# A state update in two wide operations instead of four narrow ones, r and k of two chunks scaled together, and a new written order

## The chip, the cores and the metric

The kernel runs on one core of one Trainium2 chip. The metric is the device time of one execution in microseconds (us). Three runs of the kernel before took 506.49, 506.82 and 509.15 us, median 506.82.

## The reference

Two stages, in float32. The first is a linear attention with a decaying state: for each of 4 batches and 8 heads (head size 48, 768 positions)

```
for t in range(S):
    cur = u[None] * kt  (outer)  vt
    y[t] = rt @ (state + cur)
    state = w * state + kt (outer) vt
```

The second is a feed-forward on the 3072 resulting rows of 384: `h = x @ w_in` (384 to 2048), `g = h * erf(softplus(h))`, `out = g @ w_out` (2048 to 384).

## The kernel before

The attention is computed in 24 chunks of 128 positions; a chunk of number g belongs to batch g % 4. Heads stand in four pairs: of a pair, head one lies on partitions 0 to 47 and head two on 64 to 111, so a pair fills `PR` = 112 rows. The steps of one chunk, each with a letter in the written order (the number behind the letter is the chunk's):

- `L..a`, `L..b`: SP loads the two halves of a chunk into a tile `att` (three buffers, a fourth for chunk 3). The `a` half holds r and k transposed (2 x 512 columns), the `b` half v, k and r in natural layout.
- `R`, `K`, `N` (lines 224 to 234): r, k and natural k are scaled by tables of powers of w (`wr`, `wk`, `wkn`). A `+` behind a word puts a step on POOL, a `*` on ACT, nothing on DVE.
- `A` (line 298): TensorE forms the 128x128 scores. `Qa`, `Qb`, `Qc`, `M` make the diagonal tile `am`, `P` copies the masked scores into it. Chunks 0 and 1 go another way (`G`, `V`, `Q`): line 322 masks the scores and line 338 adds the diagonal.
- `Y` (line 331): output of the chunk, from `am` and from the state `sbd`. `Xa`, `Xc`, `Xb` split it in a high and a low part for the feed-forward.
- `D` (line 356): TensorE forms the chunk's own contribution `ds` to the state, 112 rows by 4 pairs by 48 columns in PSUM.
- `S` (lines 370 to 380): the state update. The state tile `sbd` has 112 rows, 4 batches, 4 pairs and 96 columns and is block-diagonal: head one uses columns 0 to 47 of rows 0 to 47, head two columns 48 to 95 of rows 64 to 111; the rest is zero. Each update works on the two blocks apart, 48 rows and 192 columns: for chunks 0 to 3 two multiplies on DVE (`Sc`, `Sd`), for the later ones two adds on DVE (`Sa`, `Sb`) and two multiplies on DVE or POOL (`Sc`, `Sd`).

The feed-forward goes in 96 steps n of 512 rows by 128 hidden columns: `f` (line 412) 9 matmuls into a PSUM tile `h` (three buffers, which `ds` and the later `y` share), then `a b z c d e g h l` (five activations and a cast on ACT, three operations on DVE), then `p` (line 467) 9 matmuls into the accumulators. The float32 weights are fetched (`F`) and split in two parts (`Ca`, `Cc`, `Ce`, `Cf`) on the way.

All of this is put in one written order: the string `ORDER`, line 727, is read word for word, and each engine executes its instructions in that order. An instruction that waits holds back all that follow on its engine. 16 dummy matmuls run on TensorE while the first loads land (line 510, `W2` is two more).

```
pw (tables of powers)  ->  R, K  ->  A  ->  P  ->  Y  ->  X  ->  f0  ->  a0 b0 z0 c0 d0 e0 g0 h0 l0  ->  p0
```

Of the kernel before, what the change touches and what calls it, by code (L numbers as in the profile page):

```python
# [9 lines left out]
F32 = mybir.dt.float32  # L10
# [29 lines left out]
V0, K0, R0, AW = 1024, 1472, 1856, 2240  # L40
# [3 lines left out]
def body(ctx: ExitStack, tc: tile.TileContext, att, attn, wcol, ucol, u, win, wout, levels, outT):  # L44
    nc = tc.nc
# [118 lines left out]
    wr = const.tile([PR, NPAIR, C], F32, name="wr")  # L164
    wk = const.tile([PR, NPAIR, C], F32, name="wk")
# [374 lines left out]
    preps = dict(K=prep_k, R=prep_r, N=prep_n, G=prep_g)  # L540
    words = ORDER.split()
    last = max(i for i, x in enumerate(words) if x[0] == "C")
    for i, x in enumerate(words):
# [60 lines left out]
        elif what == "S":  # L604
            if sub in "ab":
                s_add(num, "ab".index(sub))
            elif num < 4:
                s_add(num, "cd".index(sub))
            else:
                s_mul(num, "cd".index(sub), eng)  # L610
# [122 lines left out]
C02a d1 e1 L7a C01f f2 N6 S4b C02c f3 g1 P50 a2 h1 P51 Y5 S4d+ M60+ F03 L7b F11 b2 z2 M61* a3 b3 C02e R6+ K6 l1 A6 Q7a
Q7b z3 X5a c2 X5b P60 d2 c3 d3 e2 e3 C11a P61 Q7c g2 C02f+ g3 M70 C11c p1 f4 h2 l2 a4 b4 C11e K7+ R7+ C11f+ M71+ N7+
Y6 D6 A7 S6b S6a f5 z4 F12 C03a X6a c4 d4 e4 a5 h3 P70 X6b C03c P71 b5 C03e C03f+ g4 l3 z5 p2 Y7 D7 C12a X7a h4 c5 d5
e5 S7b S6c+ N5+ S7a X7b C12c S4c L10a F13 F05 L8a C12e C13a p3 f6 f7 a6 C12f+ g5 l4 b6 z6 h5 l5 C13c c6 a7 d6 b7 z7 e6
g6 f8 p4 p5 f9 a8 c7 C13e h6 l6 L8b F04 b8 C05a z8 R10+ C13f d7 c8 d8 e7 e8 g7 a9 h7 g8 C05c l7 p6 f10 b9 h8 l8 C05e
p7x a10 b10 z10 z9 O70a F14 O70b p7y O71a c10 d10 c9 e10 p7z p8x f11 p8y d9 e9 O72a a11 g10 C05f+ g9 h9 C04a b11 Q8a+
Q8b Q8c l9 M80 f12 a12 z11 C04c O72b O71b F07 L10b p8z h10 l10 c11 d11 b12 z12 e11 C14a c12 p9 f13 d12 a13 e12 g11 b13
h11 g12 l11 p10 f14 f15 p11 z13 h12 l12 a14 C04e b14 z14 C04f C14c c13 d13 c14 e13 a15 d14 g13 M81 F06 b15 e14 C07a  # L740
h13 C14e g14 l13 z15 C14f p12 f16 f17 h14 a16 c15 l14 p13 d15 b16 C07c z16 e15 a17 c16 g15 h15 l15 F15 C07e d16 b17 R8
C07f K10+ K8+ e16 g16 z17 p14 p15x O150a p15y O151a D5 A8 S5b Q10a+ h16 C06a c17 d17 l16 S5a C06c C06e e17 g17 L9a
O150b f18 a18 p15z b18 f19 h17 O152a P80 l17 z18 p16x C06f+ p16y p16z f20 p17 a19 b19 c18 z19 C15a d18 P81 e18 c19 d19
g18 C15c e19 C15e h18 a20 f21 L9b O152b F16 O151b O230a O231a F17 b20 Q9a+ Q10b+ Q9b Q10c g19 h19 a21 C16a l18 C15f+
z20 l19 Q9c M90+ c20 b21 d20 e20 z21 g20 C16c f22 c21 a22 d21 e21 p18 N8 g21 p19 f23 f24 C16e h20 C16f l20 h21 b22 z22
C17a R9+ N9 l21 a23 c22 b23 K9 z23 d22 e22 c23 g22 C17c p20 d23 e23 C17e g23 h23 a24 C17f+ M91+ p21 Y8 h22 l22 X8a b24
f25 a25 A9 b25 M100* X8b l23 z24 z25 S7d+ S5d+ M101+ S5c+ c24 d24 e24 c25 d25 D8 p22 p23x L11a L11b P90 S8a P91 g24
# [12 lines left out]
X13b M151* g42 p41 D13 Y14 D14 A15 X14a h42 S13a S13b S14b l43 S14a P150 l42 f44 a44 f45 p42 b44 z44 X14b P151 p43 Y15  # L760
# [98 lines left out]
```

## Time and profile before

| | |
|---|---|
| profiled execution, its own time | 506.56 us |
| span in the profile | 504.7 us |
| PE busy | 491.9 us (97%) in 4466 matmuls |
| ACT busy | 393.0 us (78%) |
| DVE busy | 344.5 us (68%) in 622 operations |
| POOL busy | 133.8 us (27%) |
| DMA moved | 48.15 MB |
| chain that ended last | PE 87%, DVE 5%, ACT 5%, DMA 1% |

1.86 us of the execution lie outside the span. Busy shares are of the whole span; the page gives the granted clock of TensorE as full in all 40 slices. A matmul's end is modelled, so what counts on PE is when the next instruction starts and what is named as the reason of an idle time.

### The profile page before, as it was taken

The page shows a single profiled execution, that of the slowest core. Times are in us where ns is not written, and L with a number is a line of the kernel's source. Part 1 is how long each engine was busy: PE and PEld are TensorE (multiplying, and loading weights), DVE is VectorE, ACT ScalarE, POOL GpSimd, SP SyncE. Part 2 cuts the span into 40 slices and gives each one's busy share as a digit, 9 for nine tenths or more (in the row PEclk, how much of TensorE's full clock was granted, in tenths as well). Part 3 has the DMA queues.
Part 4 walks back from the last instruction along what each step waited for, and adds up shares of the span by engine and source line. Part 5 has one row for each costly group of instructions (what it writes and reads, how often), then busy time and mean ns, then how long its engine had stood idle before and what let it go on. Part 6 is the DMA issues. An engine that isn't in the chain of part 4 may idle for free.

```text
span 504.7 us, 11016 instructions
## 1 busy us (share of the span) xinstructions
PE 491.9 (97%) x4466; PEld 392.6 (78%) x4466; DVE 344.5 (68%) x622; ACT 393.0 (78%) x714; POOL 133.8 (27%) x126
## 2 busy tenths in 40 slices
PE   7899999999999999999999999999999999999995
PEld 4867887887878888887888878778878788888883
DVE  7999875687978967665777768677664444445452
ACT  1768999999986676878678875877786878988783
POOL 5755744103354453200171033436000000000000
PEclk9999999999999999999999999999999999999999
DMA  7966462436305521300430122322010000100001
GB/s 266 357 223 219 169 216 84 154 124 198 126 10 188 193 105 44 112 1 1 169 129 1 43 92 92 114 94 93 22 42 1 1 1 1 42 22 0 0 1 68
DMA packets 14136, 48.15 MB, mean 95 GB/s; under 512 B 1792, under 2 KB 2176, under 8 KB 14080
## 3 DMA queue, kind: packets, MB, share of 16 engines
q1 hardware_dynamic: 14080, 47.39, 26.8%
q8 instruction: 37, 0.61, 0.5%
q14 instruction: 19, 0.16, 0.1%
HBM read 41.09 MB, written 6.29 MB: 94 GB/s over the span
## 4 chain that ended last, share of the span: by engine, by line
PE 87%; DVE 5%; ACT 5%; DMA 1%; issue 1%; SPq 0%; DVEq 0%; ACTq 0%
PE h L419 38%; PE acc L479 37%; PE y L338 6%; PE A L309 3%; PE ds L361 1%; DMA att<-in_att_dram 1%; DVE s L435 1%; ACT s L439 1%; DVE s L451 1%; DVE gl L462 1%; ACT s L443 1%; ACT am L289 1%; ACT gh L457 1%; ACT s L447 1%; DVE am L317 1%
## 5 line engine op out<-in xcount | busy, mean ns | idle before, releaser
L419 PE MATMUL h<-x,wih 128*128 128x512 f32 x576 | 183.1, 399 | 0.6 <-ACT x L400 0.3
L419 PEld LDWEIGHTS h<-x,wih 128*128 128x128 f32 x576 | 107.4, 188 | 27.5 <-PE A L309 0.6
L479 PE MATMUL acc<-gh,woh 128*128 128x512 f32 x288 | 115.6, 401 | 0.1
L479 PE MATMUL acc<-gl,woh 128*128 128x512 f32 x288 | 114.4, 397 | 0.5 <-DVE gl L462 0.5
L419 PE MATMUL h<-x,wil 128*128 128x512 f32 x288 | 114.2, 396 | 0.0
L479 PE MATMUL acc<-gh,wol 128*128 128x512 f32 x288 | 114.1, 396 | 0.0
L451 DVE SCALAR_TENSOR_TENSOR s<-s,h 128x512 f32<-128x512 f32 x96 | 65.2, 684 | 64.6 <-ACT s L447 64.4
L462 DVE TENSOR_TENSOR gl<-s,gh 128x512 fp32r<-128x512 f32 x96 | 71.8, 754 | 42.0 <-ACT gh L457 40.1
L435 DVE SCALAR_TENSOR_TENSOR s<-s,h 128x512 f32<-128x512 f32 x96 | 65.5, 685 | 35.3 <-ACT s L430 33.5
L426 ACT ACTIVATE s<-h 128x512 f32<-128x512 f32 x96 | 56.4, 588 | 34.3 <-PE h L419 33.2
L439 ACT ACTIVATE s<-s 128x512 f32<-128x512 f32 x96 | 60.1, 627 | 29.0 <-DVE s L435 28.9
L457 ACT CAST gh<-s 128x512 fp32r<-128x512 f32 x96 | 58.5, 614 | 17.1 <-DVE s L451 12.0
L479 PEld LDWEIGHTS acc<-gh,woh 128*128 128x128 f32 x288 | 54.2, 188 | 14.6 <-issue 0.9
L479 PEld LDWEIGHTS acc<-gl,woh 128*128 128x128 f32 x288 | 54.3, 188 | 13.8 <-DVE gl L462 1.3
L419 PEld LDWEIGHTS h<-x,wil 128*128 128x128 f32 x288 | 54.2, 188 | 13.3 <-DVE wil L142 0.2
L479 PEld LDWEIGHTS acc<-gh,wol 128*128 128x128 f32 x288 | 54.2, 188 | 13.0
L430 ACT ACTIVATE s<-s 128x512 f32<-128x512 f32 x96 | 60.2, 628 | 1.6
L443 ACT ACTIVATE s<-s 128x512 f32<-128x512 f32 x96 | 60.0, 627 | 1.8
L447 ACT ACTIVATE s<-s 128x512 f32<-128x512 f32 x96 | 59.8, 627 | 1.8
L317 DVE COPY_PREDICATED am<-mask,A 64x128 f32<-64x128 uint32 (+2 forms) x108 | 37.9, 388 | 2.4 <-POOL am L530 0.9
L530 POOL TENSOR_TENSOR att<-att,ub 128x384 f32<-128x384 f32 x15 | 17.1, 1138 | 63.3 <-DMA att<-in_att_dram 62.8
L530 POOL TENSOR_TENSOR att<-att,wk 112x512 f32<-112x512 f32 x14 | 18.4, 1317 | 51.2 <-DMA att<-in_att_dram 50.4
(88 smaller groups left out, 460.9 us busy)
## 6 DMA issues: line engine op xcount, KB each, us to landing
att<-in_att_dram SPq DMA_DIRECT2D x22, 608.0 KB, 5.6
att<-in_att_dram SPq DMA_DIRECT2D x24, 512.0 KB, 3.9
raw<-in_wout_dram SPq DMA_DIRECT2D x8, 768.0 KB, 4.4
raw<-in_win_dram SPq DMA_DIRECT2D x7, 768.0 KB, 4.3
out_dram<-o SPq DMA_DIRECT2D x18, 256.0 KB, 2.3
part<-o SPq DMA_DIRECT2D x6, 256.0 KB, 3.0
o<-part SPq DMA_DIRECT2D x6, 256.0 KB, 3.4
raw<-in_win_dram SPq DMA_DIRECT2D x2, 384.0 KB, 9.0
```

What stands on the lines that cost most here:

```text
L317: nc.vector.copy_predicated(out=o, data=ap[rows, n, :, i], mask=mask[rows, n, None, i].to_broadcast(list(o.shape)).bitcast(U32))
L419: nc.tensor.matmul(out=h, lhsT=w[:, f, q, :], rhs=x[:, xi, q, :], start=k == 0, stop=k == 8)
L426: nc.scalar.activation(out=s1, in_=e["h"], func=AF.Tanh, bias=FB0, scale=FA0 * SHIFT)
L430: nc.scalar.activation(out=s1, in_=s1, func=AF.Tanh, bias=FB1, scale=FA1)
L435: nc.vector.scalar_tensor_tensor(out=e["s"], in0=e["s1"], scalar=FG / SHIFT, in1=e["h"], op0=ALU.mult, op1=ALU.add)
L439: nc.scalar.activation(out=s, in_=s, func=AF.Tanh, bias=FB2, scale=FA2 * SHIFT)
L443: nc.scalar.activation(out=s, in_=s, func=AF.Square, bias=FB3, scale=FA3)
L447: nc.scalar.activation(out=s, in_=s, func=AF.Square, bias=FB4, scale=FA4)
L451: nc.vector.scalar_tensor_tensor(out=s, in0=s, scalar=FC, in1=ff[n]["h"], op0=ALU.subtract, op1=ALU.mult, reverse0=True)
L457: nc.scalar.copy(out=e["gh"], in_=e["s"])
L462: eng.tensor_tensor(out=e["gl"], in0=e["s"], in1=e["gh"].bitcast(F32), op=ALU.subtract)
L479: nc.tensor.matmul(out=acc[e], lhsT=w[:, f, es], rhs=g, start=first and i == 0, stop=last and i == 2)
```

## The change

1. `sbd` is updated over all 112 rows and 384 columns at once. The contribution `ds` is read twice over (a broadcast over the two 48-column blocks), and the multiply uses a new table `own` that holds w to the 128th power in the own block and zero in the other, so the other block returns to zero. For chunks 0 to 3 that is one multiply (`Sc`), for the later ones one add (`Sa`, DVE) and one multiply (`Sc`, DVE or POOL). So that no row is undefined, the eight of a chunk's sixteen `ds` matmuls that have 16 columns become four of 32 and four of 16.
2. `wr` and `wk` become one tile `wrk`. Chunks 0 and 1 have r and k scaled by one operation of 1024 columns (`J`).
3. `ORDER` is written anew.

```
-    wr = const.tile([PR, NPAIR, C], F32, name="wr")
-    wk = const.tile([PR, NPAIR, C], F32, name="wk")
+    wrk = const.tile([PR, 2, NPAIR, C], F32, name="wrk")
+    wr, wk = wrk[:, 0], wrk[:, 1]
...
+    own = const.tile([PR, NPAIR, 2], F32, name="own")
+    nc.gpsimd.memset(own, 0.0)
...
+    for r, hh in ((slice(0, D), 0), (slice(H, PR), 1)):
+        nc.gpsimd.tensor_copy(out=own[r, :, hh], in_=wp[r, 7, 0])
...
+    def prep_both(g, eng):
+        t = chunks[g][:PR, 0:V0]
+        eng.tensor_tensor(out=t, in0=t, in1=wrk.rearrange("p n a c -> p (n a c)"), op=ALU.mult)
...
-            for c0, c1 in ((0, 32), (32, D)):
+            for c0, c1 in ((0, 32), (32, D if hh else H)):
...
-    def s_add(g, hh):
...
-    def s_mul(g, hh, eng):
...
+    def s_wide(g, part, eng):
+        sv = sbd[:, g % 4].rearrange("p a (n d) -> p a n d", n=2)
+        if part == "a" or g < 4:
+            ds = st_[g]["ds"][:, :, None, :].to_broadcast([PR, NPAIR, 2, D])
+        if part == "a":
+            nc.vector.tensor_tensor(out=sv, in0=sv, in1=ds, op=ALU.add)
         else:
+            eng.tensor_tensor(out=sv, in0=ds if g < 4 else sv, in1=own[:, :, :, None].to_broadcast([PR, NPAIR, 2, D]),
+                              op=ALU.mult)
...
-L0a U0 L1a L2a L0b L2b F00 L3a L1b F08 L3b B0 B0* H0 R0 K0 A0 K1 G0 V0 W2 R1 A1 R2 F10 G1+ P00 Q0 P01 K2 P10 Q2a+ Q2b+
...
+L0a L1a L2a U0 L0b L2b L3a L3b L1b F00 B0 B0* J0 A0 G0 V0 J1 P00 P01 Q0 A1 Y0 Q2a P10 P11 R2+ K2+ G1+ H0 N0* D0 X0a V1
...
```

Counted over the whole program, PE issues the same number of matmuls, `W2` included; DVE loses 38 operations, ACT 12, POOL gains 6. On ACT the diagonal tiles `M` fall from 12 to 9, each of four activations. On DVE 40 adds and first multiplies of the state become 20; the 32 later multiplies (17 on POOL, 15 on DVE) become 16 (9 and 7).

The order moves the most in front of `f0`. Three places:

On DVE, the stretch in which the states of chunks 0 and 1 are written (`sbd<-ds`), before:

```order
L261 TENSOR_TENSOR att_172<-att_172,kt_261 128x4x48 x2
L374 TENSOR_TENSOR sbd<-ds_244,wp 48x4x48
L278 TENSOR_REDUCE q_307<-att_174 128x8
L374 TENSOR_TENSOR sbd<-ds_244,wp 48x4x48
L291 TENSOR_TENSOR am_0_310<-idents,q_307 128x512
```

and now:

```order
L282 TENSOR_TENSOR att_176<-att_176 128x384
L385 TENSOR_TENSOR sbd<-ds_269,own 112x384
L286 TENSOR_REDUCE q_315<-att_176 128x8
L238 TENSOR_TENSOR att_181<-att_181,wrk 112x512
L269 TENSOR_TENSOR att_174<-att_174,kt_288 128x4x48 x2
L282 TENSOR_TENSOR att_181<-att_181 128x384
L385 TENSOR_TENSOR sbd<-ds_333,own 112x384
```

The two narrow writes around the reduce are one wide write, and the work of chunk 3 (`att_181`) has moved in between.

On ACT, the last operations in front of the first activation of the feed-forward (`x` are the halves of the attention's output, `am` the diagonal tiles, `top` a weight group), before:

```order
L289 ACTIVATE am_0_415<-idents,q_398 128x128 x4
L289 ACTIVATE am_1_420<-idents,q_398 128x128 x4
L400 CAST x_407<-y_270 128x3x128
L400 CAST x_407<-y_322 128x3x128
L130 ACTIVATE top<-raw_228 128x768
L383 CAST x_407<-y_475 128x3x128
L383 CAST x_407<-y_492 128x3x128
L400 CAST x_407<-y_475 128x3x128
L400 CAST x_407<-y_492 128x3x128
L426 ACTIVATE s_0_554<-h_544 128x512
```

and now:

```order
L297 ACTIVATE am_1_391<-idents,q_381 128x128 x4
L406 CAST x_286<-y_350 128x3x128
L140 CAST wih<-wt_384 128x384
L130 ACTIVATE top<-raw_458 128x768
L389 CAST x_286<-y_440 128x3x128
L389 CAST x_286<-y_468 128x3x128
L297 ACTIVATE am_1_524<-idents,q_511 128x128 x4
L406 CAST x_286<-y_440 128x3x128
L406 CAST x_286<-y_468 128x3x128
L140 CAST woh<-wt_518 128x768
L432 ACTIVATE s_0_563<-h_552 128x512
```

A diagonal tile of chunk 4 (`am_1_524`) now stands in front of the last two casts of `x`, and a weight group `top<-raw_458` still in front of the first two.

On SP, the loads behind the first halves of the chunks, before:

```order
L75 DMA att_174<-in_att_dram 128x1216
L120 DMA raw_178<-in_win_dram 128x1536
L71 DMA att_180<-in_att_dram 128x1024
L75 DMA att_172<-in_att_dram 128x448
L120 DMA raw_178<-in_win_dram 128x1536
L75 DMA att_180<-in_att_dram 128x1216
L120 DMA raw_228<-in_wout_dram 128x3072
```

and now:

```order
L75 DMA att_176<-in_att_dram 128x1216
L71 DMA att_181<-in_att_dram 128x1024
L75 DMA att_181<-in_att_dram 128x1216
L75 DMA att_174<-in_att_dram 128x448
L120 DMA raw_185<-in_win_dram 128x1536 x2
L71 DMA att_310<-in_att_dram 128x1024
L75 DMA att_310<-in_att_dram 128x1216
L120 DMA raw_458<-in_wout_dram 128x3072
```

Chunk 3 now comes ahead of the first weights, and chunk 4 (`att_310`, which takes over the buffer of chunk 0) ahead of the weight group `raw_458` that ACT's `top` reads.

## Rows read from the trace of the kernel before

**Rows 1.** Busy time by stage; columns: window, then PE, PEld, DVE, ACT, POOL, PEclk, DMA
```profile
8.80:27.40 18.60, 16.80 (x418) 14.66 (x417) 17.89 (x34) 11.22 (x30) 11.56 (x9) 1.00 0.91 335
27.40:41.30 13.90, 12.68 (x214) 9.05 (x213) 13.50 (x23) 8.91 (x15) 8.02 (x6) 1.00 0.66 235
41.30:317.00 275.70, 275.48 (x2565) 222.62 (x2564) 207.67 (x365) 227.30 (x410) 93.40 (x79) 1.00 0.32 111
317.00:323.00 6.00, 4.86 (x128) 3.80 (x127) 3.75 (x8) 5.39 (x12) 1.66 (x2) 1.00 0.10 17
490.00:504.70 14.70, 8.64 (x36) 6.17 (x34) 4.74 (x7) 5.80 (x10) 0.00 (x0) 0.95 0.16 58
```
**Rows 2.** Timeline of PE, head: start, us, operation xcount [idle before <-releaser]
```profile
8.84 1.16 PE L309 MATMUL A<-att 48*128 48x128 f32 x16
10.41 1.02 PE L247 MATMUL kt<-uw,att 112*128 112x2 f32 x8 [0.41 <-DVE att L239]
...
19.65 0.54 PE L361 MATMUL ds<-att 128*16 128x48 f32 x30 [1.10 <-issue]
...
24.45 1.95 PE L338 MATMUL y<-am,att 128*32 128x128 f32 x64
...
28.13 0.50 PE L419 MATMUL h<-x,wih 128*128 128x512 f32 x1 [0.29 <-ACT x L400]
...
34.52 0.86 PE L338 MATMUL y<-att,sbd 112*32 112x128 f32 x24 [0.46 <-DVE sbd L374]
...
38.11 0.50 PE L479 MATMUL acc<-gl,woh 128*128 128x512 f32 x1 [0.23 <-DVE gl L462]
...
41.30 0.63 PE L419 MATMUL h<-x,wih 128*128 128x512 f32 x2
```
**Rows 3.** Waits of PE, whole span: engine, line, waited for, us in total, times, longest
```profile
PE ds L361 <- DVE s L451: 0.9, 1, 0.9
```
**Rows 4.** Timeline of DVE, head
```profile
6.60 0.68 DVE L230 TENSOR_TENSOR att<-att,wr 112x512 f32<-112x512 f32 x1
7.20 0.68 DVE L226 TENSOR_TENSOR att<-att,wk 112x512 f32<-112x512 f32 x1
...
17.38 0.36 DVE L374 TENSOR_TENSOR sbd<-ds,wp 48x192 f32<-48x192 f32 x1
17.77 0.79 DVE L291 TENSOR_TENSOR am<-idents,q 128x512 f32<-128x512 f32 x1
...
22.16 2.62 DVE L317 COPY_PREDICATED am<-mask,A 128x512 f32<-128x512 uint32 x4 [0.25 <-PE A L309]
```
**Rows 5.** Groups by shape, whole span: operation, shapes xcount, busy us, mean ns, idle before
```profile
L530 POOL TENSOR_TENSOR att<-att,ub 128x384 f32<-128x384 f32 x15 | 17.1, 1138 | 63.3 <-DMA att<-in_att_dram 62.8
L530 POOL TENSOR_TENSOR sbd<-sbd,wp 48x192 f32<-48x192 f32 x17 | 11.3, 664 | 4.9 <-DVE sbd L376 3.7
L376 DVE TENSOR_TENSOR sbd<-sbd,ds 48x192 f32<-48x192 f32 x32 | 11.2, 350 | 2.2 <-PE ds L361 1.7
L386 DVE TENSOR_TENSOR x<-y,x 128x384 fp32r<-128x384 f32 x20 | 11.0, 550 | 1.7 <-ACT x L383 1.6
```
**Rows 6.** Timeline of ACT, head
```profile
21.54 2.45 ACT L289 ACTIVATE am<-idents,q 128x128 f32<-128x128 f32 x8
...
24.62 1.11 ACT L130 ACTIVATE top<-raw 128x768 f16<-128x768 bf16 x1
```
**Rows 7.** Busy time by stage, two later windows (columns as in rows 1)
```profile
70.00:100.00 30.00, 30.00 (x129) 24.02 (x129) 19.33 (x29) 28.69 (x52) 6.93 (x6) 1.00 0.40 140
100.00:145.00 45.00, 45.00 (x275) 35.94 (x277) 36.76 (x56) 44.33 (x77) 8.68 (x7) 1.00 0.38 126
```
**Rows 8.** DMA issues by line: KB each, median us from issue to landing
```profile
raw<-in_wout_dram SPq DMA_DIRECT2D x8, 768.0 KB, 4.4
raw<-in_win_dram SPq DMA_DIRECT2D x2, 384.0 KB, 9.0
```
**Rows 9.** Timeline of SP, the issue of chunk 4's first half
```profile
17.06 0.33 SPq L71 DMA_DIRECT2D att<-in_att_dram  x1
```

More of the change, by code (lines that the diff above doesn't have):

```diff
@@ L604, in body @@
         elif what == "S":
[L605 to L610, printed above, removed]
+            s_wide(num, sub, eng)
         elif what == "F":
@@ L733 @@
[L733 to L747, printed above, removed]
@@ new lines @@
+f16 a16 p12 c15 h14 l14 b16 d15 z16 p13 f17 C07e F15 F06 c16 e15 g15 R8+ d16 a17 h15 p14 A8 D5 b17 e16 l15 z17 g16
+C06a p15x c17 C07f+ h16 O150a C06c S5a P80 l16 d17 C06e e17 C06f+ g17 P81 Q10b O150b L9a L9b F16 p15y O151a p15z f18
+f19 f20 K9+ S5c+ R9+ a18 C15a C15c b18 z18 a19 h17 l17 O152a c18 b19 z19 p16x p16y d18 p16z p17 O151b F17 O152b O230a
+O231a e18 a20 c19 Q9a+ g18 h18 d19 e19 C15e b20 f21 l18 g19 h19 a21 C16a b21 C15f Q10c l19 z20 Q9b C16c z21 Q9c N9+
+N8+ M90+ f22 a22 c20 d20 c21 e20 d21 C16e e21 g20 g21 p18 h20 b22 l20 C16f p19 f23 f24 z22 C17a a23 h21 C17c l21 c22
@@ new lines @@
+b23 M91 z23 C17e d22 e22 p20 p21 g22 c23 d23 e23 C17f g23 h23 h22 l23 l22 f25 a25 a24 Y8 A9 b24 b25 z24 z25 X8a c24
+d24 e24 X8b P90 P91 g24 p22 p23x p23y p23z D8 h24 c25 d25 e25 Y9 O231b S8a g25 D9 X9a h25 S9a M100 M101+ S7c+ K10+ A10
+O230b l24 X9b l25 f26 f27 a26 b26 N10 z26 P100 P101 a27 b27 z27 c26 p24x p24y f28 d26 e26 c27 O231c L11a L11b O232a
+L12a O232b p24z R11+ Q11a Q11b+ d27 N11+ R12+ O230c L12b K12+ Q12a+ Q12b+ e27 g26 K11 h26 a28 g27 l26 Q11c b28 z28
+M110 c28 M111* p25 Y10 D10 A11 p26 S10a P110 P111 Y11 O232c O310a O311a L13a X10a d28 e28 h27 L13b S8c g28 X10b Q12c
@@ new lines @@
+Q16c M160+ Q17a+ M161+ g45 X15a h45 D15 A16 S15a X15b P160 l45 L18a L18b O311c f46 a46 f47 f48 b46 z46 Q17b h44 l44
+p44 p45 c46 d46 e46 a47 b47 a48 Q18a z47 N17+ S15c+ g46 Q17c N16+ c47 d47 e47 h46 b48 g47 h47 M170+ M171+ Q18b+ l46
+Q18c f49 f50 a49 b49 p46 z48 l47 p47x z49 p47y p47z c48 d48 e48 a50 c49 P161 g48 d49 e49 h48 R18+ K17+ R17+ l48 b50
+O470a g49 z50 O471a h49 l49 S13c f51 a51 b51 z51 p48x f52 p48y O470b O472a c50 c51 d50 e50 d51 e51 p48z p49 g50 g51
+h50 l50 Y16 D16 A17 L19a L19b a52 b52 S16a z52 K18 h51 X16a X16b Z0a P170 l51 c52 p50 f53 f54 d52 a53 b53 P171 e52 z53
@@ new lines @@
+c68 d68 e68 d67 e67 a69 g68 h68 g67 p66 Y23 Y22 X23a h67 X23b l68 X22a b69 X22b z69 l67 f70 f71 c69 d69 a70 b70 z70
+e69 p67 c70 d70 a71 g69 b71 h69 l69 f72 a72 z71 c71 d71 e70 p68 p69 e71 g70 g71 h71 l71 b72 h70 z72 l70 f73 Z0b f74
+p70 c72 a73 d72 e72 b73 a74 g72 Z0c z73 c73 h72 b74 d73 l72 p71 f75 O632b z74 e73 g73 c74 d74 h73 e74 a75 b75 g74 l73
+z75 c75 f76 p72 p73 f77 d75 e75 a76 g75 b76 h75 l75 h74 z76 l74 c76 d76 a77 b77 f78 z77 e76 g76 p74 f79 p75 c77 a78
+d77 e77 b78 h76 a79 g77 l76 z78 b79 c78 h77 d78 e78 l77 z79 g78 f80 a80 p76 p77 f81 b80 c79 d79 h78 l78 e79 g79 h79
@@ new lines @@
+z80 c80 d80 e80 a81 l79 g80 f82 b81 a82 p78 p79x p79y z81 b82 c81 h80 l80 O790a d81 O791a e81 z82 g81 p79z f83 p80x
+p80y f84 c82 d82 h81 a83 e82 b83 l81 g82 z83 O791b O790b O792a c83 p80z p81 f85 h82 l82 a84 b84 d83 e83 z84 g83 h83
+c84 d84 a85 b85 l83 z85 c85 d85 e84 e85 g84 g85 p82 p83 f86 a86 h84 f87 f88 b86 h85 l84 z86 l85 a87 c86 d86 a88 b88
+e86 p84 g86 h86 b87 z88 l86 z87 p85 f89 p86 c88 c87 d87 e87 d88 e88 g87 g88 f90 f91 a89 h87 l87 b89 h88 z89 l88 c89
+a90 d89 b90 z90 e89 g89 p87 c90 d90 e90 a91 b91 h89 l89 g90 p88 f92 f93 h90 a92 b92 l90 z91 z92 c91 d91 a93 e91 p89
@@ L790 @@
+g91 c92 h91 l91 d92 b93 z93 e92 g92 c93 p90 f94 f95 d93 e93 h92 l92 g93 a94 b94 z94 a95 b95 c94 p91 h93 l93 d94 z95
+p92 e94 g94 c95 h94 l94 d95 e95 g95 p93 p94 h95 l95 p95x O950a p95y p95z O792b O951a O952a O950b O951b O952b
 """
```

87 lines of the change are left out of this document (33 added, 54 removed).

## The prediction, made before the changed kernel ran

> **What bounds the kernel now.** I read the busy time by stage first, then the timeline of PE where the stages show idle time, and then the engines that PE waits for there. In the stages [rows 1] PE is idle for 1.80 us of the first 18.60 after the dummies (18.60 - 16.80), for 1.22 of the next 13.90, for 0.22 of the 275.70 that follow, and for 1.14 between 317 and 323 us. From the first scores to the last matmul that is 4.4 us. The rest of the idle time is the start, in which PE runs dummies until 8.84 us, and the 6.06 us of the last stage, mostly the way of the last output to memory. So PE, in the order in which it is told to work, is the bound; DVE, ACT and POOL matter only where PE waits for them. By the counts given with the change, PE issues as many matmuls as before. Everything that this change can win is therefore in those 4.4 us (0.9%), and 3.0 of them lie between 8.8 and 41.3 us.
>
> The timeline of PE names them [rows 2]: 0.41 us in front of the first `kt`, whose operand DVE made late; 1.10 us in the middle of `ds` of chunk 1, released by nothing that the profile shows ("issue"); 0.29 us inside `f0`, for the last cast of `x`; 0.46 us in front of `Y4`, which waits for a state write on DVE; 0.23 us in `p0`, for the low half `gl`; the rest in pieces under 0.25. At 41.30 us `f2` starts; by then PE has done `A0` to `A5`, `Y0` to `Y4`, `D0` to `D4`, `f0`, `f1` and `p0`. The new order has done exactly this set when its `f2` starts, `W2` included, so the start of `f2` is a mark at which both can be compared: what moves it is idle time alone. The 1.14 us at 317 hang on a PSUM buffer that DVE frees with a `g` step, 0.9 of them [rows 3].
>
> **The change part by part.**
>
> *One scaling for r and k.* Before: two operations of 0.68 us that overlap by 0.08 [rows 4], 1.28 together. One of 1024 columns is bounded by 1.28 and, without any saving, 1.36. It ends by 6.60 + 1.36 = 7.96 us, while PE runs dummies until 8.84 [rows 2]: nothing gained, nothing lost. Behind it the product for `kt` comes next on DVE (0.68 us, so 8.6), no longer behind chunk 1, and PE reaches `kt` at 8.84 + 1.16 = 10.0. The wait of 0.41 goes.
>
> *The wide state update.* The trace has no such operation. The nearest rows are a PSUM source of 384 columns on all rows, 0.55 us [rows 5], and a product with a broadcast operand on 512 columns, 0.79 us [rows 4]. Two narrow ones cost 2 x 0.35 = 0.70 [rows 5]. So one update costs DVE between 0.15 less and 0.09 more; I take 0.55, the row with the same columns and the same source. Over 20 updates that is 3.0 us less DVE work (bounds: 3.0 less to 1.8 more). From 41 to 317 us it hides behind PE, which has 0.22 us of idle time there [rows 1]; it costs or gives only in the head, where DVE is busy for 13.50 of 13.90 us [rows 1], and there it is four or five updates, 0.7 us. Behind a narrow write on the upper rows the trace shows no overlap: the one at 17.38 is 0.36 long and the next starts at 17.77, while two operations on all rows overlap by 0.08 [rows 4]. The Trainium skill has a rule for this ("VectorE: DVE Perf Modes", section on two Vector instructions with no wait between them): an instruction whose operands start in another quadrant of partitions than those of the one before is held until that one has finished. The trace agrees with it at this place. By that rule the head would save some 0.1 us more on each side of every second narrow write; if that reached PE in part, the sum would be some 0.3 us lower. I leave it out.
>
> The later multiplies: on POOL nine of about 1.14 us (the row with 384 columns) take the place of seventeen of 0.66, 10.3 us for 11.3 [rows 5]. They wait for nothing that PE is about to use, and POOL sits idle for most of the span. I cost them at zero.
>
> *The wider `ds` matmuls.* 20 chunks times 4, in two passes each, 160 instructions grow from 16 to 32 columns. The row of `ds` shows 30 in 0.54 us, 18 ns each, both widths mixed [rows 2]. If time went by width, they would be 24 and 12, and the change would cost 160 x 12 ns = 1.9 us on PE itself. The other end is nothing, because the 48 moving columns are the same. I take nothing, and keep 1.9 for the range.
>
> *The order in the head.* What idle time is left, if PE does the same work? (a) The 1.10 us of "issue" came among the many small matmuls of the first two chunks, and the new order issues the same ones there: I keep it. (b) `Y2` and `Y3` need four masked copies, 2.62 us on DVE [rows 4], which start when `A2` is done. Meanwhile PE has `A3` (as long as `A0`, 1.16) and `Y2` (half of 1.95 [rows 2]), together 2.1, and a subtraction of `x`; `D2` no longer stands in front. The fourth copy ends between 0 and 0.5 us after that: I take 0.25. (c) `f0` needs the low halves of `x`. On ACT there stand, from the end of `Y3`: a cast, four activations for a diagonal tile (half of 2.45, 1.23 [rows 6]), two casts; with a cast at no more than DVE's 0.55 for the same columns [rows 5] that is at most 2.9 us. PE covers `D2` 0.54 and `A4` 1.16 [rows 2] of them, 1.7 us, and two subtractions of `x` and the first matmul of `f0`. The wait lies between 0 and 1.2 us; I take 0.3, what the same matmul waited before for the same cast [rows 2]. (d) The waits of `Y4` and `p0` (0.46 and 0.23) go, since `Y4` now stands in front of `f1` but its state writes come before the first feed-forward step on DVE, and since the two dummies `W2`, which used to run while PE had to wait anyway, now stand in front of `p0` and give `gl` 0.5 us. The sum: 1.10 + 0.25 + 0.3 = 1.65 us instead of 3.02, a gain of 1.4.
>
> *Whether it is kept.* From 70 to 145 us ACT is busy for 28.69 of 30 and 44.33 of 45 us [rows 7]; it has 2.0 us to spare in 75 (1.31 + 0.67). If PE is 1.4 us early, ACT has to be as well. Counted in the two orders from `a0` to `h22`, ACT now has one diagonal tile (1.23 us [rows 6]) and one weight cast less. That is about the gain, so I count it as kept. Past 145 us nothing is priced.
>
> The profiled execution took 506.56 us, 0.26 under the median of 506.82: 506.56 - 1.4 = **505.2 us**.
>
> **The rivals.**
>
> *ACT takes it back.* ACT is nearly full up to 145 us [rows 7]. If the diagonal tile's work is not enough, PE meets its 1.4 us as waits in front of `p` steps there, and the time is that of before, 506.6. For it: 2.0 us of slack in 75. Against it: the tile and the cast that are gone.
>
> *The two odd waits do not come back.* The 1.10 us of "issue" [rows 2] and the 0.9 us for the PSUM buffer [rows 3] each happened once. In another order both may miss: 505.2 - 1.10 - 0.9 = 503.2. The Trainium skill ("Runtime: NRT & Kernel Launch", section on instruction fetch mechanics) says that an engine's program is streamed in 16 KiB blocks and that this is mostly hidden. By that rule the 1.10 us is no toll for instructions and need not return; no row here shows what PE waited for. Against this rival: (a) above.
>
> *The weight group comes late: slower.* On SP, chunk 4 now stands ahead of the weight group that ACT's `top` reads, and chunk 4 waits for the buffer of chunk 0: its issue was at 17.06 us [rows 9]. With three issues of 0.33 the weights go out at about 18.1. In front of ACT's casts of `x`, `top` started at 24.62 before [rows 6]. The landing takes 4.4 us by the same tensor's row, or 9.0 by the slowest weight row, in this stretch [rows 8]: 22.5 or 27.1. From 24.6 on each microsecond holds the casts and `f0` by as much: 27.1 gives 505.2 + 2.5 = 507.7, and with the dearer `ds` matmuls 509.6. Against it: chunk 0 is needed less long in the new order (its `Y0` stands right behind `A1`), so the issue should come earlier.
>
> **How the numbers follow.** 0.5% is 2.5 us, about what a measurement of this kernel can tell from no change. Forecast 0.38 (504.2 to 506), ACT takes it back 0.19 (506 to 507), the odd waits gone 0.27 (502.4 to 504.2), the late weights 0.16 (507 to 509.8). Faster by over 2.5 us (under 504.3): nearly all of the third and a little of the first, 0.28. Slower (over 509.3): a good half of the last, 0.09. Same: 0.63. The range leaves out the lower end of the third case and the upper part of the last: 502.6 to 508.6.
>
> **What would show it.** `f2` should start near 39.9 us instead of 41.30; the `kt` step should have no wait; an "issue" gap of about 1 us should again stand among the small matmuls before 25 us; the wide updates should take about 0.55 us on DVE and 1.14 on POOL; 32-column `ds` steps should still take 0.54. From 41 to 317 us PE should stay idle for under half a microsecond. The prediction is wrong if `f2` starts as forecast but PE waits for `gh` or `gl` later, if `top` stands waiting for a DMA before `f0`, or if idle time of over 1 us shows up past 145 us, in a part for which I priced nothing.

## The result, and the profile after

The changed kernel took 501.38 us (median of 4 runs, 500.35 to 502.27) against 507.79 for the kernel before in the same job (506.49 to 509.15): a ratio of 0.987, 95% interval 0.983 to 0.992. It is 3.8 us faster than forecast, and below the range. In the later jobs the kernel before took 506.9 to 507.5 us in the median and spread from 505 to 512 over 88 runs; the changed kernel, run again, took 501.12 (500.97 to 502.13). In those 88 runs the time goes with the mean granted clock of TensorE: the 46 with 0.996 or more took 505.97 us in the median, the 8 under 0.989 took 510.2. So there are two results: the time falls by 1.3%, and the spread falls from 7 us to under 2, as far as nine runs of the changed kernel show it (e12 below, the same kernel with its tiles 32 bytes further on, reached 503.47 in six).

The busy time by stage of the changed kernel (profiled execution: 500.35 us, span 498.5), cut as in [rows 1]:

```profile
8.80:27.40 18.60, 17.99 (x448) 15.36 (x446) 18.46 (x34) 11.79 (x32) 12.61 (x10) 1.00 0.90 337
27.40:41.30 13.90, 13.81 (x196) 10.52 (x195) 13.56 (x22) 11.07 (x18) 9.53 (x8) 1.00 0.79 307
41.30:317.00 275.70, 275.60 (x2675) 222.97 (x2674) 197.85 (x335) 224.62 (x393) 105.65 (x83) 1.00 0.31 107
317.00:323.00 6.00, 6.00 (x27) 4.82 (x27) 5.80 (x10) 3.85 (x10) 2.89 (x3) 1.00 0.55 191
```

PE is idle for 0.61 and 0.09 us in the two stages of the head (1.80 and 1.22 before), and the 1.14 us at 317 are gone. PE's timeline in the head, to be read beside [rows 2]:

```profile
8.42 1.16 PE L317 MATMUL A<-att 48*128 48x128 f32 x16
9.52 1.05 PE L255 MATMUL kt<-uw,att 112*128 112x2 f32 x8
...
21.94 0.64 PE L346 MATMUL y<-am,att 128*32 128x128 f32 x15 [0.20 <-DVE am L325]
22.90 1.40 PE L346 MATMUL y<-am,att 128*32 128x128 f32 x43 [0.32 <-issue]
...
26.53 0.89 PE L425 MATMUL h<-x,wih 128*128 128x512 f32 x2
...
29.34 0.83 PE L346 MATMUL y<-att,sbd 112*32 112x128 f32 x24
...
35.70 0.50 PE L485 MATMUL acc<-gl,woh 128*128 128x512 f32 x1
...
37.67 0.63 PE L425 MATMUL h<-x,wih 128*128 128x512 f32 x2
```

The mark, the start of `f2`, falls from 41.30 to 37.67 us (in a second profile of each kernel, taken later, it stands at 43.10 and 38.22). Of these 3.63 us, 0.42 are the earlier first scores (8.84 to 8.42), and 2.33 are idle time between matmuls (gaps over 50 ns: 3.02 before, 0.69 now). The remaining 0.9 shows from start to start alone, with those gaps left out: the 160 `ds` matmuls up to the mark take 2.75 us before and 2.25 now, the two dummies of `W2` 0.53 and 0.26. The last matmul ends 6.29 us earlier, so another 2.66 come after `f2`. The wait at 317 is 1.0 of them (two gaps, 0.15 and 0.88). The rest is no wait at all: the mean distance of the starts of neighbouring feed-forward matmuls (`f` and `p` steps, some 1,670 pairs, those over 300 ns left out) falls from 234.24 to 233.38 ns, and with 1,728 such matmuls that is 1.5 us. This mean distance is called the pitch below.

DVE's timeline in the head, and POOL's at two places of it:

```profile
8.46 1.22 DVE L230 TENSOR_TENSOR att<-att,wrk 112x1024 f32<-112x1024 f32 x1
...
14.77 0.54 DVE L385 TENSOR_TENSOR sbd<-ds,own 112x384 f32<-112x384 f32 x1
...
18.55 1.01 DVE L136 SCALAR_TENSOR_TENSOR wt<-raw,top 128x384 int32<-128x384 int32 x2
...
20.55 2.58 DVE L325 COPY_PREDICATED am<-mask,A 128x512 f32<-128x512 uint32 x4
```

```profile
8.64 3.53 POOL L536 TENSOR_TENSOR att<-att,wrk 112x512 f32<-112x512 f32 x2 [0.77 <-DVE att L247]
...
20.06 1.44 POOL L536 TENSOR_TENSOR att<-att,ub 128x384 f32<-128x384 f32 x1 [1.48 <-PE A L317]
```

The new operations by shape (busy us, mean ns), beside [rows 5]:

```profile
L536 POOL TENSOR_TENSOR sbd<-sbd,own 112x384 f32<-112x384 f32 x9 | 8.9, 992 | 3.7 <-DVE sbd L383 3.0
L383 DVE TENSOR_TENSOR sbd<-sbd,ds 112x384 f32<-112x384 f32 x16 | 8.7, 551 | 5.4 <-PE ds L369 5.4
L230 DVE TENSOR_TENSOR att<-att,wrk 112x1024 f32<-112x1024 f32 x2 | 2.4, 1222 | 0.1
L385 DVE TENSOR_TENSOR sbd<-ds,own 112x384 f32<-112x384 f32 x4 | 2.2, 544 | 0.0
```

### The profile page after: what moved, and what is told of

Same layout as the page of the kernel before. It is cut to its first block, busy times and chain, and to the rows that moved or that the text cites. A ratio compares the mean times of both kernels' runs of the same rounds, so it can differ in the third digit from the quotient of the medians.

```text
span 498.5 us, 10972 instructions
## 1 busy us (share of the span) xinstructions
PE 489.1 (98%) x4466; PEld 391.7 (79%) x4466; DVE 334.2 (67%) x584; ACT 390.6 (78%) x702; POOL 149.9 (30%) x132
## 3 DMA queue, kind: packets, MB, share of 16 engines
HBM read 41.09 MB, written 6.29 MB: 95 GB/s over the span
## 4 chain that ended last, share of the span: by engine, by line
PE 92%; DVE 4%; ACT 2%; issue 1%; DVEq 0%; ACTq 0%
PE h L425 39%; PE acc L485 39%; PE y L346 7%; PE A L317 4%; PE ds L369 1%; PE dummy L95 1%; DVE gl L468 1%; DVE am L325 1%; DVE s L457 1%; DVE s L441 1%; DVE wt L136 1%; PE kt L255 0%; ACT gh L463 0%; ACT L89 0%; ACT s L453 0%
## 5 line engine op out<-in xcount | busy, mean ns | idle before, releaser
L536 POOL TENSOR_TENSOR att<-att,wrk 112x512 f32<-112x512 f32 x28 | 41.3, 1476 | 42.3 <-DMA att<-in_att_dram 39.9
L536 POOL TENSOR_TENSOR am<-idents,q 128x512 f32<-128x512 f32 x22 | 25.4, 1156 | 54.2 <-issue 24.3
```

Of the source, the lines that this page charges most:

```text
L536: i = nc.gpsimd.tensor_tensor(**kw)
```

## The experiments

**Which part of the change brings the gain?** Four kernels mix the old and the new. All four have the changed kernel's tiles. In e1 the old order issues the wide update at the first word of each old pair; in e2 the new order keeps the narrow update and two scalings; e3 has the new order up to `f2` and the old one behind it, e4 the other way round.

```diff
 e1 (old order): - S0c Q2c S0d M20 ... S2c ... S2d
                 + S0c Q2c M20 ... S2c
 e2, s_wide:     + for hh in range(2):
                 +     r, sv, w128 = s_views(g % 4, hh)
                 +     eng.tensor_tensor(out=sv, in0=ds[r] if g < 4 else sv, in1=w128, op=ALU.mult)
 e2, order:      - J0 ... J1
                 + R0 K0 ... R1 K1
```

> The operations alone: the order of before, with the wide state update (at the place of the first of each pair), the wider ds matmuls and the table in one tile; r and k still scaled apart. If the gain is the order's: 507 us, within 1 us of before, PE idle between 8.8 and 41.3 us still 2.5 to 3.0, the wait near 317 us still there. If the gain comes from DVE being relieved in the head, where it is full: 503 to 504.5, with the waits for state writes and masked copies gone. Either way PE should again stand about 1 us at 'issue' among the small matmuls if that wait is one for instructions.

> The order alone: the new order with the narrow operations (two adds, two multiplies on 48 rows, at the place of the one wide operation; ds matmuls of 16 columns; r and k of chunks 0 and 1 in two operations each). If the gain is the order's: 501 to 502.5, PE idle in the head under 1.2 us. If it is the operations': 504 to 506.

> The new order up to the first f2, then the words that are left in the order of before, with the wide operations throughout. If the gain is made in the head: 502.5 to 504 (3.6 us at f2, less what the rest gave), f2 at about 37.7 us. If ACT, nearly full up to 145 us, takes an early start back under the old order behind it: 505 to 507, with waits of PE for gh or gl between 41 and 145 us. The wait of about 1 us near 317 us should be there again if it belongs to the old order of the rest.

> The order of before up to the first f2, then the words that are left in the new order, wide operations throughout. If the gain is made in the head: 504.5 to 506, f2 at 40.5 to 41.3 us, and the wait near 317 us gone (1.1 us). If the rest of the order carries it: 502 to 503.5.

Measured, each over 10 or 12 runs: e1 506.37 us (ratio 0.997, interval 0.994 to 1.000), e2 506.79 (0.998, 0.995 to 1.001), e3 503.59 (0.992, 0.989 to 0.995), e4 503.94 (0.993, 0.989 to 0.996). In e1 PE stands 0.98 us at "issue", as before. So neither the operations nor the order gains by itself what can be told from nothing; only together they do. By place, putting the old order back on either side of `f2` costs about half of the gain in the median. The profiles do not show two separate gains, though. The last matmul ends 454.9 to 455.1 us after the start of `f2` in the changed kernel (two profiles) and in e4, and also 454.9 us after it in e11 below, which has the old order and the narrow update there. In e3 it is 457.6, and PE waits just behind the seam of the two orders:

```profile
43.75 0.86 PE L346 MATMUL y<-att,sbd 112*32 112x128 f32 x24 [1.34 <-DVE s L457]
```

So the old order behind `f2` does not take on the early head without waits; that the new order gains there by itself isn't shown. The profiles of the narrow kernel e2 and of the next one, e5, show where the head loses: PE waits 2.9 to 3.1 us in front of `Y2`.

**Which operation does the new order need?** e5 is the changed kernel with the narrow state alone (as in e2), e6 with the two scalings alone, e7 without the two dummies `W2`. The changed kernel ran beside them again.

```diff
 e6, order: - J0 ... J1
            + R0 K0 ... R1 K1
 e7, order: - D4 W2 p0x
            + D4 p0x
```

> The changed kernel with the state update alone put back: two narrow adds or multiplies in the place of each wide one and ds matmuls of 16 columns; r and k of chunks 0 and 1 still in one operation. The order alone gave nothing, so one of the two edits must carry the head. If it is the scaling in one operation: f2 at 37.7 to 38.5 us and 501.5 to 503 us. If it is the state update: f2 at 40 us or later, a wait of PE before Y2, 504.5 to 507 us.

> The changed kernel with only the scaling put back: r and k of chunks 0 and 1 in two operations each, wide state update. If the scaling carries the head: the second half for chunk 1 runs beside POOL's first operations and is stretched (1.75 us instead of 0.68 in the order alone), the weight operations of DVE fall beside POOL's later, PE waits 2 to 3 us before Y2, f2 at 40 to 42 us, 504.5 to 506.5 us. If the state update does: 501 to 502.5 us.

> The changed kernel without the two dummy matmuls in front of p0. They cost 0.5 us on PE if gl of the first step is there by then; the trace has it ready some 0.3 us after they end, so the gain should be 0 to 0.3 us: 501.0 to 501.4, not to be told from the changed kernel. If PE's clock falls without them: 502 to 504.

> The changed kernel once more, beside the three others on the same chip. The mean distance of two feed-forward matmuls was 234.2 ns in the profile of before and 233.3 to 233.4 in five others, which is 1.4 us over the program: if that belongs to the execution and not to the kernel, this one may show either. 501 to 502 us, f2 at 37.3 to 38 us.

Measured: e5 506.49 us (12 runs, 503.73 to 508.18; ratio 0.997, 0.995 to 1.000), e6 501.09 (0.986, 0.982 to 0.991), e7 501.06 (0.986, 0.982 to 0.991), the changed kernel again 501.12 (0.987, 0.983 to 0.991), with `f2` at 38.22 us, 0.2 past what was expected. The state update is what the order needs. Scaling r and k in one operation gives nothing. Without `W2` the profile shows 0.69 us of wait in `p0` and no loss in the median.

Now the narrow kernel e5, PE's timeline, then DVE's, then POOL's:

```profile
21.33 0.55 PE L402 MATMUL y<-x,neg 128*128 128x128 f32 x3
24.93 0.41 PE L346 MATMUL y<-am,att 128*32 128x128 f32 x4 [3.05 <-DVE am L325]
```

```profile
8.65 2.29 DVE L230 TENSOR_TENSOR att<-att,wrk 112x1024 f32<-112x1024 f32 x1
...
19.18 0.71 DVE L385 TENSOR_TENSOR sbd<-ds,wp 48x192 f32<-48x192 f32 x2
...
20.39 2.65 DVE L136 SCALAR_TENSOR_TENSOR wt<-raw,top 128x384 int32<-128x384 int32 x2
...
24.14 2.58 DVE L325 COPY_PREDICATED am<-mask,A 128x512 f32<-128x512 uint32 x4
```

```profile
8.25 3.83 POOL L535 TENSOR_TENSOR att<-att,wrk 112x512 f32<-112x512 f32 x2 [1.51 <-DMA att<-in_att_dram]
...
20.36 1.00 POOL L535 TENSOR_TENSOR att<-att,ub 128x384 f32<-128x384 f32 x1 [0.25 <-DMA att<-in_att_dram]
21.44 1.19 POOL L535 TENSOR_TENSOR att<-att 128x384 f32<-128x384 f32 x1
```

The two weight operations took 2.65 us here and 1.01 in the changed kernel, with the same shapes and data. Here they start at 20.39, when POOL has been on a product of chunk 4 for 0.03 us; there they are through before POOL starts at 20.06. The scaling of chunk 1 likewise: 2.29 us where POOL's scaling started 0.40 before it, 1.22 where DVE started 0.18 before POOL, and then POOL's pair is the longer one. It looks as if one of the two engines holds something until its instruction ends, and the other stands. The Trainium skill has this rule ("SBUF — State Buffer", section on who interferes with whom): VectorE and GpSimd share one pair of ports, a VectorE instruction with two SBUF inputs contends for it with a GpSimd instruction that reads SBUF, and whichever starts first has it for its whole length. The rows agree: each longer time is the short one plus what was left of the other engine's instruction, to within 0.15 us. The two places where DVE stands in this way are called meetings below. The first meeting is not the narrow form's own: e7 and e12 (described below, the changed kernel with its tiles 32 bytes further on) show the 2.29 us too, with POOL 0.07 and 0.06 us ahead, and `f2` at 39.52 and 39.58. The second is. e12's head runs like e5's up to the first state write, at 16.04 us in both; its DVE, then its PE:

```profile
8.64 2.29 DVE L231 TENSOR_TENSOR att<-att,wrk 112x1024 f32<-112x1024 f32 x1
...
19.81 1.01 DVE L136 SCALAR_TENSOR_TENSOR wt<-raw,top 128x384 int32<-128x384 int32 x2
...
21.81 2.60 DVE L326 COPY_PREDICATED am<-mask,A 128x512 f32<-128x512 uint32 x4
```

```profile
22.59 0.41 PE L347 MATMUL y<-am,att 128*32 128x128 f32 x4 [1.12 <-DVE am L326]
```

Its weight operations start ahead of POOL's product (20.10 us), and POOL's product takes 2.66 us instead of 1.00. The narrow writes put e5's weight operations 0.58 us later, behind the start of that product; from there the difference grows to 2.33 us at the masked copies and 2.75 at `f2`.

Against the first profile of the changed kernel the masked copies start 3.59 us later. Of these, 0.19 is a later start of the scaling, 1.07 the longer scaling, 0.28 twice the narrow writes with what follows each, and 1.64 the weight operations; 0.13 is left. The granted clock then adds to it, windows of e5:

```profile
22.00:25.30 3.30, 0.36 (x4) 0.14 (x4) 3.27 (x5) 2.22 (x7) 1.87 (x2) 0.99 0.69 277
25.30:28.70 3.40, 3.21 (x65) 2.94 (x67) 3.40 (x7) 1.72 (x3) 0.00 (x0) 0.50 0.02 5
28.70:32.00 3.30, 3.30 (x81) 2.75 (x74) 3.25 (x8) 2.96 (x8) 1.16 (x1) 1.00 0.45 117
```

After the stretch in which PE was busy for 0.36 of 3.30 us, 0.50 was granted (1.2 GHz) for 3.4 us, then full speed again. e2 shows the same beside a wait of 2.88.

**Is it the meeting, or the narrow form itself?** e8 adds to the changed kernel one more DVE operation behind each of the first two state writes, in place of the narrow form's extra DVE time; e9 keeps e5's narrow state and takes the two meetings away, by two one-column copies that make POOL wait for DVE's result. A second profile of the kernel before was taken, and e10 puts 21 more matmuls in front of the first scores.

```diff
 e8, after s_wide:  + if num < 2:
                    +     zero = sbd[0:D, num, :, D:2 * D]
                    +     nc.vector.tensor_tensor(out=zero, in0=zero, in1=zero, op=ALU.mult)
 e9, word w:        + src = chunks[1][:, 0:1] if num == 1 else sums[0, 0][:, WG - 1:WG].bitcast(F32)
                    + nc.gpsimd.tensor_copy(out=seen[:src.shape[0]], in_=src)
 e9, order:         - R2+ ... Q4a+
                    + w1 R2+ ... w4 Q4a+
 e10, keep_warm(13 instead of 16):
                    + for _ in range(24):
                    +     nc.tensor.matmul(out=d[:, 0:2], lhsT=warm[:, 2:2 + P], rhs=warm[:, 0:2], ...)
```

> The changed kernel (wide state updates, new order) with one more DVE operation of 48 rows x 192 columns behind the state write of chunk 0 and of chunk 1 (it multiplies zeros by zeros in the same tile), so DVE has the 2 x 0.27 us more work that the narrow form has there, and nothing else differs. Theory A, a narrow write costs only its own DVE time and the head can carry that: f2 starts within 0.6 us of the changed kernel's profiles (37.7 to 39.5), the time is 501 to 502 us. Theory B, what costs is the lateness, because it puts DVE's weight operations beside POOL's products of chunk 4: in the profile the two weight operations take over 1 us each, PE waits over 1.5 us before Y2, f2 starts past 41 us, and the time is 504 to 506.5 us. If DVE's scaling of chunk 1 is short in this execution (1.2 us, not 2.3), B can miss in the profile and still show in the median.

> The new order with the narrow state (which took 506.49 us) and two single-column copies on POOL that read what DVE has just written: POOL waits for the scaling of chunk 1 before it scales chunk 2, and for the second weight operation before its two products of chunk 4. All work and the order on each engine stay. Theory B, the loss comes from DVE and POOL operations that run at the same time: the scaling falls from 2.29 to about 1.2 us, the two weight operations from 1.39 and 1.34 to about 0.54 each, the wait of PE before Y2 from 3.05 to under 1 us, f2 starts near 38.5 to 39.5 and the time is 502 to 503.5 us. Rival, the narrow form is slow by itself (its time and the hold between its halves): the wait before Y2 stays above 2 us and the time is 505.5 to 507 us.

> The kernel before, unchanged, for a second profile. If the matmul pitch of 234.24 ns belongs to the one execution, it is 233.3 to 233.4 here as in all others, and the last matmul then ends about 1.4 us earlier. If the 1.10 us wait in front of the second matmuls of D1 hangs on the kernel's instruction stream, it is here again, 0.9 to 1.2 us; if it was chance, it is gone. The same for the 0.9 us before D near 320 us.

> The kernel before with 13 dummy matmuls instead of 16 and 24 tiny ones of two columns behind them: 21 more matmuls ahead of the first scores, at nearly the same time. If the 1.10 us wait comes from the supply of instructions, it stands 21 matmuls earlier in the program (at about the 200th of the kernel before's count, in Y1 instead of D1) and ends about 2.5 us after a 16 KB block begins to move, or it vanishes if the matmuls there give the block time enough. If it comes from the step itself (data, buffers), it stays inside D1.

e8: 502.96 us (ratio 0.993, 0.990 to 0.996). 7 of its 12 runs lie between 501.0 and 503.1, 5 between 504.3 and 506.0; the changed kernel, e6 and e7 never passed 502.3 in 17 runs. The time lies between what the two theories gave. The profile is one of the shorter runs: no meeting, a wait of 1.05 us in front of `Y2`, `f2` at 38.84. The two added operations took 0.59 and 0.58 us there and put the weight operations 1.25 us later than in the changed kernel (19.80 for 18.55), more than twice what the narrow writes do. So 1.25 us of DVE work costs 1.8 us in the median. That fits the lateness that now and then ends in a meeting (the four longest runs had a mean granted clock of 0.991, the four shortest 0.997 to 0.998), but no longer run of e8 has a profile, so for this kernel it isn't shown.

e9: 504.01 us (0.995, 0.992 to 0.998), against 506.49 for e5. DVE and PE in its profile:

```profile
8.65 1.22 DVE L232 TENSOR_TENSOR att<-att,wrk 112x1024 f32<-112x1024 f32 x1
...
19.71 1.01 DVE L136 SCALAR_TENSOR_TENSOR wt<-raw,top 128x384 int32<-128x384 int32 x2
...
21.82 2.61 DVE L327 COPY_PREDICATED am<-mask,A 128x512 f32<-128x512 uint32 x4
```

```profile
22.61 0.41 PE L348 MATMUL y<-am,att 128*32 128x128 f32 x4 [1.23 <-DVE am L327]
```

With POOL held back both DVE times are the short ones, the wait falls from 3.05 to 1.23, the clock stays, and `f2` starts at 39.33 instead of 42.33. So the meetings, with the clock that falls behind them, are the cause of 3 us at this mark. The time misses what was expected by 0.5, and three of the twelve runs lie at 506.0 to 506.4. It stays 2.9 us above the changed kernel's; in the profiles 2.4 us of the difference lie behind `f2`. There PE still waits 0.40 and 0.52 us near 54 and 320 us for a narrow add (`sbd`), and 0.58 near 163 for DVE's copy of an output (`o`); the changed kernel has no wait of over 0.1 us there. That the narrow form costs the whole remainder by its own time is argued and not shown.

The second profile of the kernel before shows such meetings at another place, PE, DVE and POOL:

```profile
19.08 0.53 PE L361 MATMUL ds<-att 128*16 128x48 f32 x30 [1.10 <-issue]
...
36.31 0.43 PE L338 MATMUL y<-att,sbd 112*32 112x128 f32 x8 [2.22 <-DVE sbd L374]
```

```profile
30.41 2.13 DVE L291 TENSOR_TENSOR am<-idents,q 128x512 f32<-128x512 f32 x2
32.47 2.22 DVE L234 TENSOR_TENSOR att<-att,wkn 128x384 f32<-128x384 f32 x1
```

```profile
30.99 1.00 POOL L530 TENSOR_TENSOR att<-att,ub 128x384 f32<-128x384 f32 x1 [0.59 <-DMA att<-in_att_dram]
32.44 1.83 POOL L530 TENSOR_TENSOR wol<-wt,woh 128x768 fp32r<-128x768 f32 x1 [0.45 <-ACT woh L140]
```

In this execution the pair of diagonal tiles met POOL's product, and the next operation (0.54 us alone, 1.37 beside POOL in the first profile) stood for the length of POOL's subtraction; PE waited 2.22 us for the state write, where [rows 2] has 0.46. The time was 508.56 us. The granted clock stayed full. So such meetings can be one source of the spread of the kernel before. Its longest runs, of 510 us and more, all had a mean granted clock of 0.993 or less, and none of them has a profile.

The profile also answers three other things: the pitch is 234.23 ns again, the 1.10 us of "issue" stand in front of the same matmul, and the 0.88 us near 320 are there again. e10 (507.65 us in one run) answered nothing: among the tiny matmuls the granted clock fell to 0.50 from 10.9 to 21.1 us, and a PE at half speed had no wait of "issue" there.

**The pitch, and the wait of "issue".** The change adds a table `own` of 32 bytes per partition in front of the states. Every tile allocated behind it (states, chunks, x, gl, gh) moves by 32 bytes: gh, for one, from 96 past a multiple of 128 to a multiple of 128. e11 gives the kernel before that shift alone; e12 shifts the changed kernel by 32 more; e13 repeats e10's question with 37 dummies of 221 columns for 16 of 512.

```diff
 e11, e12: + pad = const.tile([PR, 8], F32, name="pad")
             sbd = const.tile([PR, 4, NPAIR, 2 * D], F32, name="sbd")
 e13:      - nc.tensor.matmul(out=d, lhsT=warm[:, 2:2 + P], rhs=warm[:, 0:TB], ...)
           + nc.tensor.matmul(out=d[:, 0:221], lhsT=warm[:, 2:2 + P], rhs=warm[:, 0:221], ...)
           - WARM = 16
           + WARM = 37
```

> The kernel before with one unused tile of 32 bytes per partition in front of the state tile, where the changed kernel has its new table of that size: everything allocated behind it (the states, the chunks, x, gl, gh) moves by 32 bytes and then starts at multiples of 64, as in the changed kernel. Theory A, the place of the operands sets the pitch: the feed-forward matmuls fall from 234.24 ns to 233.3 to 233.4, and the time by about 0.9 ns x 1700 = 1.5 us, to 505 to 506.3 against the kernel before in the same job. Theory B, the pitch hangs on the narrow or wide code or on the order: it stays at 234.2 and the time does not move by more than 0.5 us.

> The changed kernel with one unused tile of 32 bytes per partition behind its new table, so that the states, the chunks, x, gl and gh start at odd multiples of 32 again. Theory A: pitch 234.2 ns, time 1.5 us more than the changed kernel, 502.5 to 503.3. Theory B: pitch 233.4, 501 to 501.7.

> The kernel before with 37 dummies of 221 columns in place of 16 of 512: nearly the same columns at the start, 21 matmuls more. If the 1.10 us of issue comes from the supply of instructions, it stands 21 matmuls earlier (in the count of the kernel before near its 199th, inside Y1), and ends about 2.5 us after a 16 KB block of instructions begins to move. If it belongs to D1 (data, a buffer), it stays in front of D1's third matmul.

The mean distance between neighbouring feed-forward matmuls, with the place of gh past a multiple of 128:

```
gh at 96: before 234.24, before again 234.23, e10 234.23, e13 234.22 ns
gh at 0:  after 233.38, after again 233.38, e1 233.32, e5 233.41, e11 233.32 ns
gh at 32: e12 233.30, e9 233.29 ns
```

e11 took 505.76 us against 507.21 (ratio 0.997, 0.993 to 1.001): in its profile the last matmul ends 454.9 us after `f2`, as in the changed kernel, and not 457.6. The 1.0 us near 320 are gone there too, but also in e10 and e13, which keep the old order, the narrow update and the old places: so that wait isn't the old order's by itself, and what brings it stays open. In e10 and e13 the last matmul ends 456.3 and 456.2 us after `f2`, with as much idle time as in e11 (0.54 to 0.58 us), so the profiles give the pitch 1.4 us. The move alone sets the pitch; pitch times matmuls gives 1.5 us, and the measured 1.45 has an interval that reaches nothing. e12 refutes my rule for it: odd multiples of 32 do not bring 234.2 back (501.24 us, pitch 233.30). Which property of the place counts stays open. e1 to e9 all carry the move (e9's added tile moves gh on to 32), so they are better read against e11, though it ran in another job: from its 505.76 e1 and e2 gain nothing, e3 2.2 us, e4 1.8 and the whole change 4.5. No kernel of the study beat the changed one by more than its spread.

e13 (506.16 us in one run), PE's timeline:

```profile
18.39 0.74 PE L339 MATMUL y<-idents,att 128*32 128x128 f32 x18 [1.06 <-issue]
...
23.95 0.66 PE L398 MATMUL y<-x,neg 128*128 128x128 f32 x4 [1.22 <-issue]
```

Counted from the first dummy, the first wait stood in front of the 221st matmul before and stands in front of the 220th here, though that is now in `Y1` and not in `D1`: it goes by the count of matmuls, not by the step. The trace's transfers of instructions say why: blocks of 16 KB begin to move at 15.99 and 21.38 us, and the waits end at 18.39 and 23.95, 2.4 and 2.6 us later (before: 17.07 and 19.65; after: 20.46 and 22.90). That fits a PE that waits if it runs through what it has left in less time than that: before, it was through 1.5 us after the block's start. In all 17 profiles every "issue" wait of over 0.15 us in the first 45 us stands in front of matmul 220 or 221, 347 or 348, or 601. The second profile of the changed kernel has two of them:

```profile
17.79 0.70 PE L346 MATMUL y<-am,att 128*32 128x128 f32 x17 [0.26 <-issue]
...
23.36 1.40 PE L346 MATMUL y<-am,att 128*32 128x128 f32 x43 [0.56 <-issue]
```

## Why the prediction was wrong, by its steps

- **"Everything that this change can win is therefore in those 4.4 us."** This step failed. It took every matmul to cost what it cost before. The new table moved the operands, and the 1,728 feed-forward matmuls follow each other 0.9 ns closer (e11), which is worth 1.4 to 1.5 us. The sum had no term for a 32-byte table.
- **The wide update: "there it is four or five updates, 0.7 us".** The durations were right (551 and 544 ns for 0.55; on POOL 992 for 1.14), the price was not. The step summed DVE's own time, and the sum at the end has no term for it. In the new order the narrow form makes DVE late enough to meet POOL's products of chunk 4, and the 0.6 us of two updates grow to 2.3 at the masked copies and 2.75 at `f2` (e5 against e12), 5.4 us in the median (e5 against the changed kernel, with what the narrow form costs behind `f2`). The step also took the waits of the kernel before as fixed: the 0.46 of `Y4` is 2.22 in another execution.
- **(a) The 1.10 us of "issue" kept.** This failed too. The step reasoned that the same small matmuls are there; the wait goes by the count of matmuls and by what PE does in the 2.5 us behind a block's start (e13). In front of matmul 221 PE stood 1.10 us before, and nothing or 0.26 in the two profiles of the changed kernel; in front of 347 or 348 it stood 0.17 in the first profile, and now 0.32 or 0.56. The rival with the odd waits gone said 503.2 and came nearest, but by luck in part: it had no term for the pitch, and the wait at 317 went in kernels with the old order too. The Trainium skill's sentence that this fetch is mostly hidden ("Runtime: NRT & Kernel Launch", instruction fetch mechanics) holds for the many later blocks; here two of the first ones cost up to 1.1 and 1.2 us.
- **The wait of `kt`** went, as forecast. **(b)** forecast 0.25, measured 0.20 and 0.21; that is luck in part, since with the same order and the wide update PE waits another 0.93 us (e6) and 1.12 (e12) for these copies where the scaling of chunk 1 took longer. **(c)** forecast 0.3, measured under 0.05: ACT was ready for `f0`. **(d)** held in the first profile: no wait in `Y4` and none in `p0`; the second has 0.18 in `p0`.
- **Costs at nothing.** One scaling: right (e6). Wider `ds` matmuls: right, 32 and 16 columns take the same (0.32 to 0.34 us from the first start to the last of a chunk's 32 where PE does not wait, in both kernels), and none of the 1.9 us came. `W2`: no price (e7).
- **Whether it is kept.** Right: from 41.3 to 317 us PE is idle for 0.10 us. ACT did not take it back. With the old order behind `f2` some of it is taken back, though not by ACT: e3's 1.34 us hang on DVE.
- **The late weights** did not come: chunk 4 was issued at 14.21 us, 2.85 earlier than in [rows 9], as the argument against that rival had it, the weights behind it at 15.05 instead of 18.1, and `top` waited for no DMA:

```profile
14.21 0.33 SPq L71 DMA_DIRECT2D att<-in_att_dram  x1
...
15.05 0.43 SPq L120 DMA_DIRECT2D raw<-in_wout_dram  x1
```

```profile
22.33 1.11 ACT L130 ACTIVATE top<-raw 128x768 f16<-128x768 bf16 x1
```

So head and rest were both undersized: 1.4 us forecast at `f2`, 3.63 measured (3.08 to the second profile of the changed kernel); nothing forecast behind it but the 317 wait of a rival, 2.66 measured.

## What to carry to other kernels

An operation on DVE is not priced by its own duration where POOL runs beside it: look which of the two starts first wherever they meet, and take the profile's wait as one draw from a race, above all where runs spread. Split a change in two before crediting either half; here neither order nor wide update gained alone. And when a change adds or removes any tile, compare the spacing of a long run of equal matmuls first: it may have moved all operands.

## What the runs showed of the hardware that I had not expected

A two-input DVE operation took 1.22 or 2.29 us for the same shape, depending on who started first: 2.29 where POOL's was 0.06 to 0.40 us ahead (e5, e7, e12), 1.22 where DVE's was 0.18 to 0.90 us ahead (the changed kernel, e8). A shift of 32 bytes moved the matmul pitch from 234.24 to 233.32 ns, a further 32 did not move it back. Beside a wait of about 3 us PE's granted clock fell to 0.50 for 3.4 us (e2, e5); in e7 two waits of 0.50 and 0.35 us came before such a stretch (12.0 to 15.5 us), in e11 one of 1.40 us before a longer one (20.8 to 27.7 us), while waits of 1.05 to 2.22 us in the kernel before (both profiles), e3, e4, e8, e9, e12 and e13 had none behind them. And where PE waited for a block of instructions, the wait ended 2.3 to 2.6 us after the block's transfer began (before, both profiles of the changed kernel, e11, e13).
